# Attention in two halves a pair: four switches of TensorE's tiling, sums inverted one pair on, a new order of SyncE's transfers

## The chip, the core and the metric

The kernel runs on one core of a Trainium2 chip. A core has five engines that run side by side: TensorE (PE, matrix products; PEld is its loading of weights), VectorE (DVE), ScalarE (ACT), GpSimd (POOL) and SyncE (SP), which here only issues transfers (DMAs). PE's results go to PSUM, a small memory, and VectorE and ScalarE read them there. The other on-chip memory is SBUF, with 128 partitions. The metric is device time in microseconds; less is better.

## The reference

Two blocks follow each other. The first is attention with a hash mask, over 4 batches, 8 heads, 768 positions and a head size of 64; the second is a feed-forward over the 3,072 tokens of 512 that come out of it.

```python
q_bits = np.einsum('bhsd,dk->bhsk', q, proj) > 0        # 6 bits of a hash, for k too
mask = q_bucket[:, :, :, None] == k_bucket[:, :, None, :]
scores = np.where(mask, q @ k.T / sqrt(D), -1e9)
attn = exp(scores - max) / (sum + 1e-9)
x = attn @ v                                            # (B,H,S,D) -> (B*S, H*D)
h = x @ w_in                                            # 512 -> 2048
out = (h * sigmoid(1.702 * h)) @ w_out                  # 2048 -> 512
```

The weights of the feed-forward come as 64-bit floats and are converted on the chip.

## The kernel before

**Pairs.** Attention goes over 16 pairs of heads, n from 0 to 15, in the loop of `attention` that starts at line 648. The 128 partitions hold the two heads' 64 dimensions. Scores are made transposed: keys on the partitions, in six tiles of 128 keys (`kt`), queries along the row, in two halves of 384 (`c`). For a tile of keys and a half of queries, PE first adds a product of hash features (bf16; lines 497 and 514), which makes the masked ones hugely negative, and then the product of k and q. ScalarE takes the exponential of the result into `es[c]` (line 486).

**Tilings of PE.** PE can be split into independent smaller arrays. From pair 3 on (`BY_PARTS`), `scores_of_four` (line 500) makes two tiles of keys at once, a *group*: four products that each use 32 rows of the array (32*128 in the profile). For this a second copy of k and q exists, `other`, in which the halves of the dimensions are exchanged (`exchange`, line 439), and a second copy of the hash features (`spread`, line 479). Pairs 0 to 2 use 64 rows (64*128). The values (`values`, line 540), the hashes (`hashed`, line 455) and the sums of the exponentials (`total`, line 561) use 32 columns of the array (128*32). Each pass from one kind to the other switches the tiling.

**PSUM slots.** Scores, values, hashes and sums take turns in four slots of two 512-word places a partition (`in_turn`, line 310). One tile of keys takes a whole slot, values take half of one, and the hashes or the sums can take its other half. A slot can be used again when those that read it are done.

**One pair before.** PE's order in pair n is: two groups of scores; the values of the second half of pair n−1; two groups; the values of the first half of pair n; two groups; the hashes of pair n+2 and the sums of pair n−1. That is six switches. VectorE turns the raw k and q into columns (`turn`), adds up the exponentials (`add_high`; GpSimd adds the lower three tiles, `add_low`), makes the hash features from the hashes (`featured`), inverts the sums of pair n−2 (`invert`, line 571, which first transposes them, line 575, and then takes reciprocals) and multiplies the output by them (`norm`). It also converts one chunk of weights a pair, in six steps (`convert`, called by `begin` and `step`). ScalarE, beside the exponentials, unloads the values (`unload`, lines 558 and 559) and sums squares for a guard (`measure`, line 451).

**SyncE's row.** All transfers of attention but the weights' go through `load` (line 339, issued at line 340). SyncE issues them one after the other and waits at each for what it needs. A pair has 24: four for the next k, four for the next q (`fetch`), two for the values (`fetch_v`, one a head), eight for the hash features of pair n+1 (from `f` to their places, line 471), four for the exchange of halves of pair n+1 and two for the second copy of its features. The last two copy what the eight wrote, and wait until it has landed. From pair 2 on they are kept in the order of the program; before that the scheduler places them.

**Order.** The order of the work on PE, VectorE, ScalarE and GpSimd is that of the program text; a release of a buffer or slot is a wait on a semaphore. After attention comes the feed-forward, which uses products of the Strassen kind and is not touched by the change.

Of the kernel before, what the change touches and what calls it, by code (L numbers as in the profile page):

```python
# [38 lines left out]
def kernel(  # L39
# [249 lines left out]
    def attention(ff):  # L289
# [4 lines left out]
        with actx:  # L294
# [42 lines left out]
            turns_kept = [False]  # L337

            def load(out, in_):
                dma = nc.sync.dma_start(out=out, in_=in_)  # L340
                if turns_kept[0]:
                    tc.keep_in_program_order(dma)
                return dma
# [6 lines left out]
            def behind(x):  # L350

                nc.vector.memset(x, 0.0)

            def fetch(n, name):
# [3 lines left out]
                if (n, name) == (2, "q"):  # L358
                    behind(x[:, 0, 0:1])
# [7 lines left out]
            def fetch_v(n):  # L367
                b, hp = pairs[n]
                x = ld.tile([P, T, 2, D], F32, tag="v", name="v", bufs=2)
                if n == 0:  # L370
                    x = x.rearrange("p t j d -> p (t j d)").rearrange("p (j t d) -> p t j d", j=2, d=D)
                vts[n] = x
                if n == 1:
                    behind(x[:, 0, :, 0])
# [104 lines left out]
            def spread(n):  # L479

                exchange(n)
# [58 lines left out]
            def values(n, c, kts, at):  # L540
                av, vt = at[:, 0 : HS + 1], vts[n]
                avs[n, c] = av
                for t in kts:
                    row = t if n else 2 * (t % GT) + t // GT
                    for j in range(2):
                        for d in range(0, D, 32):
                            nc.tensor.matmul(av[D * j + d : D * j + d + 32, :], vt[:, row, j, d : d + 32], es[c][:, t, j, :],  # L547
                                             start=(t == 0), stop=(t == T - 1))
# [80 lines left out]
            fetch(2, "k")  # L629
            scores(0, 1, low, slots)  # L630
            turn(1, "q")
            add_high(0, 0)
            add_low(0, 1)
            measure(1, "q")
# [4 lines left out]
            fetch(2, "q")  # L639
            fetch_v(1)  # L640
            scores(0, 1, high, slots)
            measure(2, "k")
# [3 lines left out]
            turns[0] = 0  # L646
            inverse = {}
            for n in range(1, last + 1):

                more = n + 2 <= last  # L650
                if n > 1:
                    if n < last:
                        features = featured(n + 1)
                        next(features)
                    if n > 2:
                        inverse[n - 2] = invert(n - 2)
                        next(inverse[n - 2])
# [851 lines left out]
```

## Time and profile before

| | us |
|---|---|
| median of 3 runs | 859.17 |
| lowest and highest of them | 855.86, 860.81 |
| the profiled execution's own time | 857.29 |
| its span | 855.5 |

The clock granted to PE was 0.999 over the span. A row of the order of time shows the start and the length in us, the engine, the line, the operation, output and inputs, the shapes and the count; in brackets stands the idle time before it and what ended it. Neighbouring instructions of a kind are merged in one row. "s" is a PSUM slot, "feat" the hash features, "own" and "s_in" the columns of k and q and their exchanged copy (both names stand for either, since they rotate through three places), "e" the exponentials, "rt" the transposed sums, "acc" the added exponentials. SPq and ACTq rows are issues of DMAs.

| stretch of the span (us) | what is in it |
|---|---|
| 0 to 66.6 | pairs 0 to 2, without the 32-row tiling |
| 66.6 to 294.1 | pairs 3 to 14 |
| 294.1 to 317.4 | pair 15 and the last sums |
| 317.4 to 855.5 | feed-forward |

### The profile page before, as it was taken

Reading aid. Unit: us, or ns where it says so; the run is one execution under the profiler, and the core shown is the slowest. Engines: PE = TensorE matmul, PEld = TensorE weight load, DVE = VectorE, ACT = ScalarE, POOL = GpSimd, SP = SyncE. Lnnn points to the kernel's source line nnn. Section 1 sums busy time; section 2 is a strip of 40 time slices with the busy share of each in tenths; the row PEclk is TensorE's granted clock in tenths of the full one; section 3 lists DMA queues with packets and bytes.
Section 4 is the critical chain, followed back from the end, with each engine's and each line's share of the span. In section 5 each row is a group of like instructions: output and inputs, shape, how many; then the busy total and the mean of one; then the engine's idle time right before and its main releaser. Section 6 shows DMA issues by size and latency. Waiting matters only on the chain.

```text
span 855.5 us, 14892 instructions
## 1 busy us (share of the span) xinstructions
PE 843.9 (99%) x5595; PEld 524.7 (61%) x5595; DVE 683.9 (80%) x1069; ACT 337.6 (39%) x553; POOL 361.8 (42%) x321
## 2 busy tenths in 40 slices
PE   8999999999999999999999999999999999999997
PEld 4444444444444444565666666545888888888886
DVE  4479889988878986788887788676998977897786
ACT  6666665667666644343444444433000000000000
POOL 4333343433433448997854467568664100000000
PEclk9999999999999999999999999999999999999999
DMA  5657866776777403526466546577854675467534
GB/s 112 98 91 150 152 137 134 158 138 130 155 146 142 114 3 135 161 81 264 188 230 221 214 155 213 205 265 269 278 174 154 205 244 194 157 222 233 193 120 100
DMA packets 165197, 144.04 MB, mean 168 GB/s; under 512 B 124384, under 2 KB 139872, under 8 KB 159872
## 3 DMA queue, kind: packets, MB, share of 16 engines
q1 hardware_dynamic: 154640, 111.22, 47.6%
q10 hardware_dynamic: 10480, 31.81, 11.8%
q8 instruction: 45, 0.74, 0.4%
q14 instruction: 32, 0.26, 0.1%
HBM read 79.69 MB, written 50.33 MB: 152 GB/s over the span
## 4 chain that ended last, share of the span: by engine, by line
PE 89%; SPq 3%; DMA 3%; ACT 1%; DVE 1%; issue 1%; POOL 1%; ACTq 0%; DVEq 0%; POOLq 0%
PE product L1232 30%; PE product L905 23%; PE s L547 12%; PE s L514 12%; PE small L973 6%; SPq L340 3%; PE product L973 3%; DMA feat<-feat 1%; PE s L497 1%; DMA q<-in_q_dram 1%; ACT e L486 1%; PE s L569 1%; PE s L461 1%; DVE acc L538 0%; POOL above L334 0%
## 5 line engine op out<-in xcount | busy, mean ns | idle before, releaser
L486 ACT ACTIVATE e<-s 128x768 f32<-128x768 f32 x192 | 143.7, 812 | 62.2 <-PE s L514 46.6
L547 PE MATMUL s<-e,v 128*32 128x385 f32 x1536 | 131.6, 488 | 0.0
L525 POOL TENSOR_TENSOR t_x<-e 128x768 f32<-128x768 f32 x32 | 55.2, 1724 | 137.5 <-ACT e L486 132.0
L905 PE MATMUL product<-xT,w_in_sb 128*128 128x512 f32 x216 | 100.0, 593 | 0.1
L547 PEld LDWEIGHTS s<-e,v 128*32 128x32 f32 x1536 | 47.2, 109 | 79.1 <-issue 60.3
L905 PE MATMUL product<-t_x,s_in 128*128 128x512 f32 x192 | 89.5, 593 | 0.0
L514 PE MATMUL s<-s_in 32*128 32x384 f32 x816 | 79.9, 482 | 0.0
L525 POOL TENSOR_TENSOR t_x<-t_x,e 128x768 f32<-128x768 f32 x32 | 55.9, 1747 | 55.7 <-ACT e L486 54.6
L538 DVE TENSOR_TENSOR acc<-acc,e 128x768 f32<-128x768 f32 x63 | 73.6, 1168 | 2.8 <-ACT e L486 0.6
L1268 ACT COPY u<-product 128x256 f32<-128x256 f32 x20 | 7.4, 372 | 158.1 <-PE product L1232 124.9
L905 PEld LDWEIGHTS product<-xT,w_in_sb 128*128 128x128 f32 x216 | 41.0, 190 | 35.7 <-issue 32.7
L905 PEld LDWEIGHTS product<-t_x,s_in 128*128 128x128 f32 x192 | 36.5, 191 | 29.8 <-issue 26.7
L514 PEld LDWEIGHTS s<-s_in 32*128 32x128 f32 x816 | 41.1, 185 | 19.8 <-issue 1.9
L514 PE MATMUL s<-own 32*128 32x384 f32 x432 | 45.6, 487 | 0.0
L921 DVE TENSOR_TENSOR u<-product,u 128x256 f32<-128x256 f32 (+1 forms) x60 | 28.4, 486 | 15.5 <-PE product L973 12.9
L466 DVE TENSOR_SCALAR f<-s,above,weight 128x384 bf16<-128x384 f32 x15 | 10.1, 676 | 32.9 <-PE s L569 25.0
L1232 PE MATMUL product<-raw_g,xT 128*128 128x256 f32 x152 | 35.1, 380 | 0.0
L514 PE MATMUL s<-feat 32*128 32x384 bf16 x312 | 30.4, 327 | 2.5 <-DMA feat<-feat 2.0
L226 POOL TENSOR_TENSOR v<-c,v 128x1024 f32<-128x1024 f32 (+1 forms) x15 | 32.3, 2156 | 1.0
L225 POOL TENSOR_TENSOR u<-v,u 128x1024 f32<-128x1024 f32 (+1 forms) x11 | 23.8, 2166 | 20.2 <-ACT v L918 14.1
L921 DVE TENSOR_TENSOR v<-product,v 128x512 f32<-128x512 f32 x24 | 16.5, 689 | 19.5 <-PE product L905 19.5
L535 DVE SCALAR_TENSOR_TENSOR acc<-t_x,e 128x768 f32<-128x768 f32 x31 | 29.4, 947 | 3.1 <-ACT e L486 2.5
(298 smaller groups left out, 1801.1 us busy)
## 6 DMA issues: line engine op xcount, KB each, us to landing
raw_g<-g_dram SPq DMA_DIRECT2D x20, 1024.0 KB, 5.1
s_in<-g_dram SPq DMA_DIRECT2D x20, 1024.0 KB, 5.0
g_dram<-c ACTq DMA_DIRECT2D x18, 512.0 KB, 2.9
raw<-in_moe_w_out_dram ACTq DMA_DIRECT2D x16, 512.0 KB, 3.7
raw<-in_moe_w_in_dram ACTq DMA_DIRECT2D x15, 512.0 KB, 5.2
s_in<-own SPq DMA_DIRECT2D x36, 192.0 KB, 3.3
v<-in_v_dram SPq DMA_DIRECT2D x32, 192.0 KB, 3.8
k<-in_k_dram SPq DMA_DIRECT2D x60, 96.0 KB, 3.1
```

The source lines that it names most:

```text
L226: lambda: eng.tensor_tensor(b12, b22, b12, op=Alu.subtract),
L340: dma = nc.sync.dma_start(out=out, in_=in_)
L486: nc.scalar.activation(es[c][:, kt, :, 0:HS], ps[:, :, 0:HS], Act.Exp, scale=1.0 / D**0.5)
L514: nc.tensor.matmul(ps[i][:, j, 0:HS], a[r0 : r0 + 32, keys], m[r0 : r0 + 32, cols], start=at == 0, stop=at == 2)
L525: nc.gpsimd.tensor_tensor(low_sum, low_sum if i else e[:, 0], e[:, i + 1], op=Alu.add)
L535: nc.vector.scalar_tensor_tensor(acc, terms[0], T * TINY, terms[1], op0=Alu.add, op1=Alu.add)
L538: nc.vector.tensor_tensor(acc, acc, terms[i + 1], op=Alu.add)
L547: nc.tensor.matmul(av[D * j + d : D * j + d + 32, :], vt[:, row, j, d : d + 32], es[c][:, t, j, :], start=(t == 0), stop=(t == T - 1))
L905: nc.tensor.matmul(ps, wq[LEFT[i]][:, kc, :], xq[RIGHT[i]][:, kc, :], start=(start and kc == 0), stop=(kc == K2 - 1), skip_group_check=not ...
L921: nc.vector.tensor_tensor(dst, x, y, op=Alu.add)
L973: nc.tensor.matmul(x, wq[LEFT[i]], xq[RIGHT[i]], start=start, stop=True, skip_group_check=True)
L1232: nc.tensor.matmul(ps, wq[LEFT[i]][:, c, :], gq[RIGHT[i]][:, c, :], start=(onto is None and c == 0), stop=(c == F4 - 1), skip_group_check= ...
```

## The change

It rewrites the order of the loop over pairs, and of what precedes it.

- A pair has two halves: three groups of scores of the first half of queries, then the values of the second half of pair n−1 with the sums of pair n−1 behind them in the same slot; three groups of the second half, then the values of the first half of pair n with the hashes of pair n+2 behind them in the same slot. That is four switches of tiling.
- The sums of pair n−1 are inverted and applied in pair n, and not in pair n+1.
- k, q, their turns and their measures move to earlier places: `measure(n+3, "k")` at the end of pair n, both turns of pair n+2 near its start. The exchange of halves is made for pair n+2 and not for pair n+1 (`exchange` is called apart from `copied`, which is what is left of `spread`).
- The values of two heads come in one transfer, and lie as head, row, dimension in SBUF.
- All transfers of `load` are kept in the order of the program from the start. In a pair this is: eight features of pair n+1, k of n+3, two copies of features of n+1, q of n+3, values of n+1, exchange of n+2.
- The two memsets that held transfers back (`behind`) are gone.
- Before the loop, the hashes of pair 2 and the sums of pair 0 are made behind pair 0's last values.
- After the loop, the norm of pair 14 and the last step of the conversion are gone, since they are done in pair 15.

```diff
             def fetch_v(n):
                 b, hp = pairs[n]
...
-                for j in range(2):
-                    order = "(t p) d -> p t d" if n else "(p t) d -> p t d"
-                    load(x[:, :, j, :], v[b, 2 * hp + j].rearrange(order, p=P))
+                x = vts[n] = ld.tile([P, 2, T, D], F32, tag="v", name="v", bufs=2)
+                heads = v[b, 2 * hp : 2 * hp + 2]
+                if n:
+                    load(x.rearrange("p j t d -> p (j t) d"), heads.rearrange("j (t p) d -> p (j t) d", p=P))
...
-            def spread(n):
-
-                exchange(n)
+            def copied(n):
+
                 for j in range(2):
                     load(both[n % 2][D * j + 32 : D * j + 48], both[n % 2][D * j : D * j + 16])
...
+            hashed(2, at[:, 1])
+            at = place(0)
+            total(0, at[:, 0])
+            turns[0] = 1
             for n in range(1, last + 1):
...
+                scores_of_four(n, ((0, 0), (0, 2), (0, 4)))
+                add_low(n, 0)
+                if more:
+                    turn(n + 2, "k")
+                    turn(n + 2, "q")
...
+                    if more3:
+                        fetch(n + 3, "k")
+                    if BY_PARTS <= n + 1 <= last:
+                        copied(n + 1)
+                    if more:
+                        measure(n + 2, "q")
+                    if more3:
+                        fetch(n + 3, "q")
+                step(n, 2)
+                add_high(n, 0, (0,))
+                step(n)
+                if n > 1:
+                    at = in_turn()
+                    values(n - 1, 1, every, at[:, 0])
+                    total(n - 1, at[:, 1])
+                    unload(n - 1, 1)
+                    inverse = invert(n - 1)
+                    next(inverse)
+                if n < last:
+                    fetch_v(n + 1)
+                if more and n + 2 >= BY_PARTS:
+                    exchange(n + 2)
+                step(n, 2)
+                add_high(n, 0, (1,))
+                next(inverse)
+                scores_of_four(n, ((1, 0), (1, 2), (1, 4)))
+                add_low(n, 1)
+                norm(n - 1)
+                add_high(n, 0, (2,))
...
+                step(n)
+                at = in_turn()
+                values(n, 0, every, at[:, 0])
+                if more:
+                    hashed(n + 2, at[:, 1])
+                unload(n, 0)
```

More of the change, by code (lines that the diff above doesn't have):

```diff
@@ new lines, in attention @@
+                more, more3 = n + 2 <= last, n + 3 <= last
+                if n < last:
+                    features = featured(n + 1)
+                    next(features)
+                if n == 1:
+                    inverse = invert(0)
+                    next(inverse)
+                else:
+                    add_high(n - 1, 1)
+                chunk = begin(n)
+                if n < last:
+                    first = next(features)
+                    if chunk is not None:
+                        behind_issue(chunk, first)
+                        behind_issue(next(features), chunk)
+                    whole(features)
@@ L764, in attention @@
                 f()
-            norm(last - 1)
-            step(last)
             inverse = invert(last)
```

141 lines of the change are left out of this document (26 added, 115 removed).

## The prediction

> **What bounds the kernel now.** I read the page first, then the windows, then the order of time on each engine. The page's first part says that TensorE (PE) is never free; the windows then give the attention's pairs 3 to 13 (66.62 to 276.19), one undisturbed pair among them (12), and pair 14.
>
> ```profile
> span 855.5 us, 14892 instructions
> PE 843.9 (99%) x5595; PEld 524.7 (61%) x5595; DVE 683.9 (80%) x1069; ACT 337.6 (39%) x553; POOL 361.8 (42%) x321
> 66.62:276.19 209.57, 207.07 (x2556) 93.97 (x2553) 178.71 (x255) 138.89 (x231) 77.08 (x44) 1.00 0.75 145
> 239.16:257.68 18.52, 18.52 (x237) 8.29 (x234) 15.54 (x23) 12.60 (x22) 7.26 (x4) 1.00 0.73 144
> 276.19:294.07 17.88, 17.88 (x230) 8.02 (x227) 17.00 (x22) 10.43 (x17) 6.23 (x4) 1.00 0.45 110
> ```
>
> Columns: window, length, busy time of PE, PEld, DVE, ACT, POOL, granted clock, DMA share, GB/s. Eleven pairs at 18.52 would be 203.72; they took 209.57, so 5.85 us are waits. The largest is shown in PE's and SyncE's order of time: pair 7's scores wait for a copy of the hash features that SyncE issued only at 141.12.
>
> ```profile
> 144.52 0.67 PE L514 MATMUL s<-feat 32*128 32x384 bf16 x2 [2.02 <-DMA feat<-feat]
> ```
>
> ```profile
> 141.12 1.53 SPq L340 DMA_DIRECT2D feat<-feat  x2
> ```
>
> ```profile
> SPq L340 <- DMA q<-in_q_dram: 8.3, 11, 1.4
> ```
>
> The last row is of SyncE's waits (us, times, longest): its row is held up by loads of q that have not landed, and the features stand behind them.
>
> **Prices of the pieces on PE**, from one undisturbed pair and from pairs 2 and 15:
>
> ```profile
> 246.19 0.34 PE L514 MATMUL s<-feat 32*128 32x384 bf16 x4
> ...
> 247.66 0.33 PE L514 MATMUL s<-feat 32*128 32x384 bf16 x4
> ...
> 249.21 4.09 PE L547 MATMUL s<-e,v 128*32 128x385 f32 x48
> 253.23 0.34 PE L514 MATMUL s<-feat 32*128 32x384 bf16 x4
> ...
> 254.69 0.33 PE L514 MATMUL s<-feat 32*128 32x384 bf16 x4
> ...
> 256.25 0.52 PE L461 MATMUL s<-s_in,pf_k 128*32 128x384 f32 x2
> ...
> 256.92 0.83 PE L569 MATMUL s<-acc,ones 128*32 128x384 f32 x8
> 257.68 0.34 PE L514 MATMUL s<-feat 32*128 32x384 bf16 x4
> ```
>
> ```profile
> 45.17 0.52 PE L461 MATMUL s<-own,pf_k 128*32 128x384 f32 x2
> ...
> 45.96 0.80 PE L497 MATMUL s<-feat 64*128 64x384 bf16 x2
> ...
> 304.32 4.09 PE L547 MATMUL s<-e,v 128*32 128x385 f32 x48
> 308.22 0.83 PE L569 MATMUL s<-acc,ones 128*32 128x384 f32 x8
> ...
> 310.45 0.45 PE L514 MATMUL s<-feat 32*128 32x384 bf16 x4
> ...
> 312.11 4.09 PE L547 MATMUL s<-e,v 128*32 128x385 f32 x48
> ...
> 317.24 1.88 PE L905 MATMUL product<-xT,w_in_sb 128*128 128x512 f32 x4
> ```
>
> Starts subtracted: a group of scores (two tiles of keys) 1.46 (254.69 − 253.23); a group with the switch to another tiling behind it 1.55 (249.21 − 247.66), so that switch is 0.09; values followed by scores 4.02, values followed by sums in the same tiling 3.90, so the switch back is 0.12; hashes before sums 0.67, sums before scores 0.76, hashes before scores 0.79. A pair before is 3 × (1.46 + 1.55) + 2 × 4.02 + 0.67 + 0.76 = 18.50; the window says 18.52.
>
> **The change, part by part.**
>
> *Four switches.* A pair is now twice: three groups, then one set of values with the sums or the hashes straight behind it. 2 × (2 × 1.46 + 1.55) + 2 × 3.90 + 0.76 + 0.79 = 18.29. That saves 0.23 a pair, if nothing waits.
>
> *What waits then.* Scores rotate through four PSUM slots, two to a group, so a third group in a row needs the slots of the first, which ScalarE must have read. Before, values always stood between. ScalarE's order of time:
>
> ```profile
> 247.87 1.51 ACT L486 ACTIVATE e<-s 128x768 f32<-128x768 f32 x2 [0.77 <-PE s L514]
> ```
>
> The first group ends at 247.66 and both its exponentials are read at 249.38, 1.72 later. A third group wants its second slot 1.46 after the first group's end: 0.26 too early. A release takes some hundredths more: at 310.45 a group wanted a slot that VectorE's transpose left at 310.50 (row below), and its values came 1.66 behind it instead of 1.55, a wait of 0.11 where 0.05 was owed. So 0.31 a half, 0.62 a pair, and a pair is 18.91. The bounds: 0, if the pair of matmuls that needs no late slot hides it; and 0.48, if its four streams also fall out of step, by half of what the late ones at 144.52 lost (0.67 against the 0.34 at 246.19). I take the middle, whose rows are nearest.
> The Trainium skill, "TensorEngine Tiling (Array Packing)", section PSUM Bottleneck, warns that tiling speeds up TensorE and not the reading of PSUM, which may become the limit; it speaks against putting three groups in a row, and the row above agrees with it. By it the sum is the one below; were there slots enough it would be 846.5.
>
> *Sums inverted one pair on.* The denominators of pair n−1 are now summed behind the values of the same half, in the same PSUM tile; the transpose that reads them runs after ScalarE has unloaded the values. Pair 15 already does this:
>
> ```profile
> 309.92 0.58 DVE L575 STREAM_TRANSPOSE rt<-s 128x384 f32<-128x384 f32 x1 [0.42 <-ACT xT L559]
> ```
>
> It comes 0.93 after the scores' start (308.22 + 0.77 = 308.99) and frees the slot at 310.50, while the second group wants it at 310.45. The 0.05 to 0.11 is not added: the third group's wait counts from the exponentials, which do not move. The hash features now share such a tile too and so start 0.93 into the pair; the cover is the same wait, and the features have the rest of the pair to land. The work of VectorE is the same, 15.54 a pair; queued behind its transpose stand one step of the weights' conversion, one sum and the inversion, and PE waits for none of these.
>
> *SyncE's row; values in one transfer.* A pair issued 8 feature copies, 4 exchanges of halves, 2 copies of features, 4 + 4 of k and q, 2 of values: 24; now 23. From the listings of SyncE's line and of the issues:
>
> ```profile
> L340 SPq DMA_DIRECT2D feat<-f x96: 507/580/4372, 71.9 to 281.8; - x96
> ```
>
> ```profile
> q<-in_q_dram SPq DMA_DIRECT2D x44, 96.0 KB, 5.5
> feat<-f SPq DMA_DIRECT2D x96, 12.0 KB, 3.1
> feat<-feat SPq DMA_DIRECT2D x24, 48.0 KB, 3.2
> ```
>
> At 0.58 each that is 13.9 before and 13.3 after, and 0.58 saved is off the path as long as SyncE has slack. New order, from the pair's start: features 1.6 to 6.3 (their source is ready after 0.93 + 0.6); k to 8.6; the copies, which wait until the features have landed (6.3 + 3.1 = 9.4), to 10.6, landed 13.8; q to 12.9; values 13.5; the exchange of the pair after next, held by q's landing, until about 16.7. Scores need the copies at 18.9: 5 us to spare, where before the four transfers of the exchange stood between the features and these copies. The exchange gets a whole pair more. I therefore take the 5.85 us of waits as gone. If that cover fails, they come back.
>
> *The start.* The hashes of pair 2 and the denominators of pair 0 move ahead of pair 1, before whose scores the sums must be ready:
>
> ```profile
> 25.42 4.20 PE L547 MATMUL s<-e,v 128*32 128x385 f32 x48
> 29.55 0.34 PE L497 MATMUL s<-feat 64*128 64x384 bf16 x2
> ...
> 36.12 4.18 PE L547 MATMUL s<-e,v 128*32 128x385 f32 x46
> ...
> 54.50 0.34 PE L497 MATMUL s<-feat 64*128 64x384 bf16 x2
> ...
> 57.84 4.09 PE L547 MATMUL s<-e,v 128*32 128x385 f32 x48
> ```
>
> ```profile
> 28.47 2.02 DVE L538 TENSOR_TENSOR acc<-acc,e 128x768 f32<-128x768 f32 x2
> ```
>
> Eight untiled key tiles take 6.57, four 3.34, so each further one 0.81; twelve are 9.80 and six 4.96. Values from 25.42 to 29.43 (they took 0.11 too long there), hashes to 30.10, sums wait for VectorE's 30.49 (0.45 lost): 31.31; twelve tiles 41.11; values 45.01; hashes 45.80; six tiles 50.76; values 54.66; sums 55.42; six tiles 60.38; values and hashes 65.07. Pair 3 began at 66.62: 1.55 gained, its waits for features (at 45.96 0.80 stands for 0.34) among them.
>
> **The sum.** Start −1.55. Pairs 3 to 13: 11 × 18.91 = 208.01, −1.56. Pair 14 has no hashes: 18.91 − 0.79 + 0.12 = 18.24, +0.36. Pair 15, to the product at 317.24, was 23.17 and is 2 × (4.47 + 0.31) + 3 × 3.90 + 0.76 + (317.24 − 312.11 − 3.90 = 1.23) = 23.25, +0.08. The feed-forward behind it is the same. Together −2.7 on the profiled execution's 857.29: 854.6. That execution is 1.9 below the median of the runs shown (859.17), which spread from 855.86 to 860.81; late features are the likely part of that spread, so no offset is added.
>
> **The rivals.** Within 0.5% is 4.3 us, about what a measurement of this kernel can tell: 854.9 to 863.5.
> 1. *No wait for the third group.* For it: PE can run the half of the group whose slot is free. Against: matmuls go out in order, and at 310.45 the wait showed in full. 26 waits × 0.31 = 8.1 less: 846.5.
> 2. *The features stay late.* SyncE's waits are for landings, and the DMA share of 0.75 does not fall. The 5.85 comes back: 860.4. With uneven restarts alone (26 × 0.17) it would be 859.0. Against: 5 us of slack by the issues.
> 3. *Slower: VectorE becomes the bound.* Its adds stretch while GpSimd adds:
>
> ```profile
> 135.47 1.92 POOL L525 TENSOR_TENSOR t_x<-e 128x768 f32<-128x768 f32 x1 [4.65 <-ACT e L486]
> ```
>
> ```profile
> 135.91 2.30 DVE L538 TENSOR_TENSOR acc<-acc,e 128x768 f32<-128x768 f32 x1
> ...
> 139.02 0.91 DVE L538 TENSOR_TENSOR acc<-acc,e 128x768 f32<-128x768 f32 x1
> ```
>
> That is 1.39 lost. The transposes of a pair's sums must be out early in its second half, and of 18.91 VectorE works 15.54; of the 3.4 left some 1.2 (an estimate, from the 0.93 above and the feature's start) are pauses for PE that it can't use: 2.2 of slack. Two such losses a pair (2.78) exceed it by 0.6, and 13 × 0.6 brings 862.4; three (4.17) exceed it by 2.0: 880. It decides against the change from 2.9 a pair on. Against: the undisturbed pair's 15.54 has its stretches in already. The Trainium skill, "SBUF — State Buffer", section Who interferes with whom, calls this an exclusive lock for a whole instruction, which these rows bear out.
>
> **How the numbers follow.** My sum 0.52 (851 to 859 with its own bounds, and with its middle just at the edge of what can be told: 0.28 of it faster, 0.24 same); rival 1 0.12, faster; rival 2 0.21, same; rival 3 0.15, slower. Faster 0.40, same 0.45, slower 0.15. The range goes from rival 1's 846.5 to 862, past rival 2, and leaves out most of rival 3.
>
> **What would show it.** Undisturbed pairs of 18.9 with no wait for a DMA; the third group of a half starting 0.3 late, and values 4.8 after a half's start; pair 3 at 65.1; SyncE idle some 2 us before each row of features. A pair of 18.3 is rival 1; PE waiting on features, rival 2; VectorE without idle time before its hash features, rival 3. Wrong too, if the feed-forward does not take the same time.

## The result, and the profile after

The changed kernel takes 862.33 us (median; 861.49 to 865.63), the kernel before, run on the same chip between its runs, 858.33. The ratio is 1.0051 with an interval of 1.0027 to 1.0076: slower by half a per cent. The prediction said 854.6 with a range that ended at 862.0, and gave "slower" 0.15. The profiled execution took 863.15.

The page's first part after the change, to be set beside that of before:

```profile
span 861.3 us, 14838 instructions
PE 847.7 (98%) x5595; PEld 529.3 (61%) x5595; DVE 691.8 (80%) x1067; ACT 342.3 (40%) x553; POOL 368.4 (43%) x321
```

The windows (length, busy time by engine, granted clock, DMA share, GB/s) of pairs 3 to 13, of one undisturbed pair, of pair 14, of the first half of pair 2, and of 3.41 us in that half:

```profile
71.81:281.32 209.51, 209.51 (x2556) 98.22 (x2553) 189.22 (x253) 141.21 (x229) 80.37 (x44) 1.00 0.68 142
128.95:148.00 19.05, 19.05 (x237) 8.94 (x235) 17.20 (x23) 12.90 (x21) 7.31 (x4) 1.00 0.71 147
281.32:300.08 18.76, 18.37 (x229) 8.75 (x226) 17.54 (x22) 11.04 (x17) 7.88 (x4) 1.00 0.25 62
48.34:57.51 9.17, 6.72 (x41) 3.30 (x37) 4.77 (x6) 4.36 (x7) 2.51 (x2) 0.82 1.01 181
...
54.19:57.60 3.41, 3.41 (x16) 1.58 (x19) 0.98 (x1) 2.76 (x4) 2.60 (x2) 0.50 0.88 221
```

By stages, from the starts of PE's work:

| | before | predicted | after |
|---|---|---|---|
| pair 3 begins | 66.62 | 65.07 | 71.81 |
| pairs 3 to 13 | 209.57 | 208.01 | 209.51 |
| pair 14 | 17.88 | 18.24 | 18.76 |
| pair 15, to the first product | 23.17 | 23.25 | 23.06 |
| feed-forward | 538.26 | 538.26 | 538.16 |

The eleven middle pairs, at which the change aims, take what they took before; they have no wait for transfers any more, but each is 0.53 longer than an undisturbed pair of before. The loss is in the start. PE's order of time there:

```profile
32.44 0.52 PE L448 MATMUL s<-s_in,pf_k 128*32 128x384 f32 x2 [1.94 <-ACT xT L545]
...
54.19 0.50 PE L483 MATMUL s<-feat 64*128 64x384 bf16 x2 [2.45 <-ACT e L472]
54.46 1.51 PE L483 MATMUL s<-s_in 64*128 64x384 f32 x4
```

and ScalarE's, which both waits name:

```profile
29.47 0.86 ACT L438 ACTIVATE xT<-k 128x768 f32<-128x768 f32 x1
...
30.45 0.84 ACT L438 ACTIVATE xT<-q 128x768 f32<-128x768 f32 x1
...
31.46 0.93 ACT L545 ACTIVATE xT<-s,vs 128x384 f32<-128x384 f32 x1
...
52.89 0.34 ACTq L165 DMA_DIRECT2D raw<-in_moe_w_in_dram  x1
53.33 3.62 ACT L472 ACTIVATE e<-s 128x768 f32<-128x768 f32 x5 [4.09 <-DMA k<-in_k_dram]
```

The first wait: the hashes of pair 2 share a PSUM tile with the last values of pair 0 and are written in the program behind the unload of these values; the unload stands on ScalarE behind two measures. The second: ScalarE stands at the issue of the first chunk of weights until a load of pair 4's k has landed (at 52.87), with exponentials behind it, and PE has no free slot. When PE goes on, its clock is halved for 3.41 us (the last window; the row of 1.51 above has four streams that take 0.81 otherwise).

ScalarE stood at that issue before the change just as long:

```profile
52.40 0.35 ACTq L165 DMA_DIRECT2D raw<-in_moe_w_in_dram  x1
52.86 1.51 ACT L486 ACTIVATE e<-s 128x768 f32<-128x768 f32 x2 [3.80 <-DMA k<-in_k_dram]
```

There PE lost nothing, because it was in the values from 50.48 to 54.50. The change put the values behind all six tiles of the half, so that the cover came too late.

### The profile page after: what moved, and what is told of

Its sections match the earlier page's. It is cut to its first block, busy times and chain, and to the rows that moved or that the text cites. A ratio compares the mean times of both kernels' runs of the same rounds, so it can differ in the third digit from the quotient of the medians.

```text
span 861.3 us, 14838 instructions
## 1 busy us (share of the span) xinstructions
PE 847.7 (98%) x5595; PEld 529.3 (61%) x5595; DVE 691.8 (80%) x1067; ACT 342.3 (40%) x553; POOL 368.4 (43%) x321
## 4 chain that ended last, share of the span: by engine, by line
PE 93%; ACT 2%; DVE 2%; DMA 1%; POOL 1%; issue 1%; SPq 0%; ACTq 0%; POOLq 0%; DVEq 0%
PE product L1190 29%; PE product L863 22%; PE s L500 14%; PE s L533 14%; PE small L931 6%; PE product L931 3%; PE s L483 2%; ACT e L472 1%; PE s L555 1%; PE s L448 1%; DMA k<-in_k_dram 1%; DVE acc L524 0%; SPq L339 0%; DVE t_x L225 0%; ACT xT L545 0%
## 5 line engine op out<-in xcount | busy, mean ns | idle before, releaser
L472 ACT ACTIVATE e<-s 128x768 f32<-128x768 f32 x192 | 145.9, 810 | 38.4 <-PE s L500 23.6
L500 PE MATMUL s<-s_in 32*128 32x384 f32 x816 | 83.2, 485 | 0.0
L511 POOL TENSOR_TENSOR t_x<-t_x,e 128x768 f32<-128x768 f32 x32 | 62.3, 1946 | 2.5
L500 PEld LDWEIGHTS s<-s_in 32*128 32x128 f32 x816 | 45.1, 185 | 14.1 <-issue 0.2
L500 PE MATMUL s<-own 32*128 32x384 f32 x432 | 49.2, 496 | 0.0
L500 PEld LDWEIGHTS <-feat 32*128 32x128 bf16 x312 | 13.4, 92 | 43.1 <-issue 37.9
L500 PE MATMUL s<-feat 32*128 32x384 bf16 x312 | 37.6, 326 | 0.5 <-DVE rt L561 0.4
L879 DVE TENSOR_TENSOR c<-small,c 128x256 f32<-128x256 f32 (+1 forms) x54 | 24.2, 462 | 9.2 <-PE small L931 9.0
```

The lines of the kernel that those rows point to most:

```text
L472: nc.scalar.activation(es[c][:, kt, :, 0:HS], ps[:, :, 0:HS], Act.Exp, scale=1.0 / D**0.5)
L500: nc.tensor.matmul(ps[i][:, j, 0:HS], a[r0 : r0 + 32, keys], m[r0 : r0 + 32, cols], start=at == 0, stop=at == 2)
L511: nc.gpsimd.tensor_tensor(low_sum, low_sum if i else e[:, 0], e[:, i + 1], op=Alu.add)
L879: nc.vector.tensor_tensor(dst, x, y, op=Alu.add)
```

## The experiments

Times and ratios are against runs of the kernel before on the same chip (medians 856.9 to 857.9; the changed kernel's own ratio was 1.0051); pairs are read from the traces, one execution of each kernel.

### Is the pair's extra time the third group's wait?

The exponentials of a half's first two tiles are taken for one head only, so that ScalarE hands these slots back earlier; the other head's part is left out:

```diff
-                        weigh(n, c, k0 + i, ps[i])
+                        weigh(n, c, k0 + i, ps[i], 1 if k0 == 0 else 2)
```

> The changed kernel with the exponentials of the first two tiles of keys of each half made for one head only from pair 3 on (the other head's exponentials of these tiles stay those of an earlier pair, so that part of the attention is left out). ScalarE then has read the slots of a half's first group 0.8 us earlier. Theory A (the third group of a half waits for ScalarE's reading of the first group's second slot): the 0.39 us that a half loses falls to what its second group waits for its slot, 0.15 in the first half and 0.05 in the second, so a pair goes from 19.05 to about 18.5 and the kernel loses some 7 us. Rival C (the loss is PE's own: three groups in a row without a change of tiling run out of step): a pair stays at 19.05.

Measured, in a single execution: 856.17. First PE's order in an undisturbed pair of the changed kernel (starts of the three groups, of the values, and the same in the second half):

```profile
128.95 0.34 PE L500 MATMUL s<-feat 32*128 32x384 bf16 x4
...
130.41 0.54 PE L500 MATMUL s<-feat 32*128 32x384 bf16 x4
...
132.02 0.56 PE L500 MATMUL s<-feat 32*128 32x384 bf16 x4
...
133.81 4.09 PE L533 MATMUL s<-e,v 128*32 128x385 f32 x48
...
138.47 0.34 PE L500 MATMUL s<-feat 32*128 32x384 bf16 x4
...
139.94 0.45 PE L500 MATMUL s<-feat 32*128 32x384 bf16 x4
...
141.45 0.66 PE L500 MATMUL s<-feat 32*128 32x384 bf16 x4
...
143.33 4.09 PE L533 MATMUL s<-e,v 128*32 128x385 f32 x48
```

then the first half of this experiment:

```profile
125.44 0.34 PE L500 MATMUL s<-feat 32*128 32x384 bf16 x4
...
126.90 0.54 PE L500 MATMUL s<-feat 32*128 32x384 bf16 x4
...
128.50 0.39 PE L500 MATMUL s<-feat 32*128 32x384 bf16 x4
...
130.11 4.09 PE L533 MATMUL s<-e,v 128*32 128x385 f32 x48
```

In the changed kernel the third group takes 1.79 and 1.88 (133.81 − 132.02, 143.33 − 141.45) where 1.55 is due, the second 1.61 and 1.51 where 1.46 is due: 0.39 too much in each half. With less work for ScalarE the third group falls to 1.61, the pair to 18.60. So 0.45 a pair is ScalarE's release of the slots, shown. The 0.15 in front of the second group stays. It belongs to the slot that the values share with the hashes, or with the sums in the second half: in the changed kernel VectorE reads that slot until 130.57 and 139.99, and the second group wanted it at 130.41 and 139.94. VectorE's and ScalarE's order of time there:

```profile
129.89 0.68 DVE L453 TENSOR_SCALAR f<-s,above,weight 128x384 bf16<-128x384 f32 x1 [1.31 <-ACT xT L545]
...
139.41 0.58 DVE L561 STREAM_TRANSPOSE rt<-s 128x384 f32<-128x384 f32 x1 [0.25 <-ACT xT L545]
```

```profile
130.69 4.69 ACT L472 ACTIVATE e<-s 128x768 f32<-128x768 f32 x6 [0.83 <-PE s L500]
...
140.21 3.02 ACT L472 ACTIVATE e<-s 128x768 f32<-128x768 f32 x4 [0.83 <-PE s L500]
```

In the changed kernel this delay adds nothing to the time: it is 0.15 in one half and 0.05 in the other, and both halves lose the same 0.39. The third group's late slot counts from the first group's exponentials, and these begin 1.74 after the half's start in both (128.95 to 130.69, 138.47 to 140.21). The delay shows only where ScalarE is quicker, as in this experiment.

### Can the start be put right?

Three kernels, one edit, the other, and both. The first puts the hashes ahead of the unload:

```diff
-            unload(0, 1)
             hashed(2, at[:, 1])
+            unload(0, 1)
```

> The changed kernel with pair 2's hashes put ahead of ScalarE's unload of pair 0's second values instead of behind it. Theory A (the time before pair 3 is lost to PE waiting for ScalarE in two places): the 1.9 us wait of PE ahead of these hashes goes, PE waits only for the sums of pair 0 (VectorE, ready at 31.4), pair 1 starts 1.6 us earlier than 33.87, and the kernel is 1.6 us faster than the changed one, about 860.7. Rival B (the start is bound by the landing of k and q, and every wait taken away comes back at the next one): pair 3 starts at 71.8 as before and the time stays 862.3.

The second issues the first chunk of weights at the end of pair 1:

```diff
-                chunk = begin(n)
+                chunk = None if n == 2 else begin(n)
...
                 if n == 1:
+                    begin(2)
                     for x in "kq":
                         measure(3, x)
```

> The changed kernel with the first chunk of weights issued one pair earlier, at the end of pair 1's exponentials, instead of ahead of pair 2's. Theory A: ScalarE no longer stands 4.1 us at this issue, PE's wait of 2.5 us in pair 2 goes and with it the 3.4 us of half clock that follow it, pair 2 takes 19.3 instead of 23.5 and the kernel is 4.2 us faster than the changed one, about 858.1. Rival B: pair 2 still waits, for q of pair 4 or the features of pair 3, and the time stays within 1 us of 862.3. If only the wait and not the clock counts, the gain is 2.5.

> The changed kernel with both of these edits. Theory A: the gains add, 5.8 us less than the changed kernel, 856.5, which is about 2 us below the kernel before; pair 3 starts at 66.0. Rival B: little is gained, above 860.

Measured: 862.51 (ratio 1.0058, 1.0037 to 1.0079), 863.57 (1.0067, 1.0046 to 1.0087) and 860.97 (1.0034, 1.0015 to 1.0052). PE's largest wait in the start, in the three kernels in turn:

```profile
53.72 0.51 PE L483 MATMUL s<-feat 64*128 64x384 bf16 x2 [4.60 <-ACT e L472]
```

```profile
63.88 0.34 PE L483 MATMUL s<-feat 64*128 64x384 bf16 x2 [3.34 <-DVE rt L561]
```

```profile
61.05 0.34 PE L483 MATMUL s<-feat 64*128 64x384 bf16 x2 [2.94 <-DVE rt L561]
```

The gain of each edit showed at its own place (pair 1 began 2.6 earlier in the first, of which 0.96 is that its first scores began earlier; the first half of pair 2 ran without a wait in the second) and was gone some microseconds on. With the hashes early, PE comes sooner to ScalarE's wait for k. With the chunk early, PE comes to a transposition of sums that stands on VectorE behind the turn of pair 4's q; VectorE's order of time in the second kernel:

```profile
59.57 0.98 DVE L424 STREAM_TRANSPOSE own<-q 128x768 f32<-128x768 f32 x1 [1.65 <-DMA q<-in_q_dram]
```

So the fourth mend adds to both that it turns that q half a pair later, with its measure, the next load of q and the exchange:

```diff
                     turn(n + 2, "k")
-                    turn(n + 2, "q")
+                    if n != 2:
+                        turn(n + 2, "q")
...
                 next(inverse)
+                if n == 2:
+                    turn(4, "q")
                 scores_of_four(n, ((1, 0), (1, 2), (1, 4)))
```

> The changed kernel with three edits: pair 2's hashes ahead of ScalarE's unload, the first chunk of weights issued one pair earlier, and, new, in pair 2 alone the turn of pair 4's q put behind the inversion of the sums instead of near the pair's start (its measure, the load of pair 5's q and pair 4's exchange follow it). Theory A2 (the start is a chain of engines that stand in order at work whose load has not landed: first ScalarE at the chunk, then VectorE at the turn of q, and PE waits for whatever stands behind): with the turn out of the way the transposed sums are in time, the wait of 2.9 us in pair 2's second half goes with the half clock behind it, pair 3 starts at 65.5 instead of 69.9 and the kernel is 4.3 us faster than with the first two edits alone, 856.7, level with the kernel before. Rival B (the loads bound the start whatever stands in front): pair 3 starts at 69.9 still, about 861.

Measured: 860.43 (1.0034, 1.0014 to 1.0053). Pair 3 began at 66.36, 5.45 sooner than in the changed kernel; but ScalarE then stood at the second chunk, in pair 3:

```profile
71.17 0.34 PE L500 MATMUL s<-feat 32*128 32x384 bf16 x2 [1.05 <-ACT e L472]
```

```profile
69.87 0.33 ACTq L165 DMA_DIRECT2D raw<-in_moe_w_in_dram  x1
```

The fifth keeps the early hashes and the late q, and issues the first two chunks behind the exponentials of their half:

```diff
-                chunk = None if n == 2 else begin(n)
+                chunk = None if n in (2, 3) else begin(n)
...
                 scores_of_four(n, ((0, 0), (0, 2), (0, 4)))
+                if n in (2, 3):
+                    begin(n)
```

> The changed kernel with its start mended as in the run that turned pair 4's q later (hashes of pair 2 ahead of the unload, pair 4's q in the second half of pair 2), but the first two weights chunks (pairs 2 and 3) are issued on ScalarE behind the exponentials of the pair's first half, so that no exponential stands behind an issue that waits for a landing. Theory: pair 3 again begins at about 66.4, and the 1.4 that PE waited for ScalarE in pair 3 (issue of the second chunk at 69.87, exponentials after 3.06 idle) are gone; pairs of 19.05 from there. Pair 4 at about 86, that is 1.6 below the 860.4 of that run: 858.8, and what is then left over the kernel before with the new row and the values in one transfer (856.4) is 11 times the 0.5 of the undisturbed pair less the start's gain. Rival: the start's wait moves once more, to a later pair: 860.4 or more.

Measured: 862.03 (1.0072, 1.0048 to 1.0095). The rival held. The chunk now lands late, VectorE's conversion waits for it, and the transposed sums behind that conversion hold PE:

```profile
81.68 0.34 PE L500 MATMUL s<-feat 32*128 32x384 bf16 x2 [2.90 <-DVE rt L561]
```

Of the 6.7 between the predicted and the measured start of pair 3, the best of these mends kept 3.2 up to pair 5 (106.66 instead of 109.90), and 0.78 of that is that the first scores began at 9.77 instead of 10.55. Each took its own wait away and made or uncovered another.

### The parts of the change alone, on the kernel before

The new order of SyncE's row alone (the exchange of pair n+2 behind q, the copies behind k; the first exchange in pair 1); the values in one transfer alone; both:

```diff
                         if n + 1 >= BY_PARTS:
-                            spread(n + 1)
...
                     if n + 3 <= last:
                         fetch(n + 3, "k")
+                    if BY_PARTS <= n + 1 <= last:
+                        copied(n + 1)
...
                         fetch(n + 3, "q")
+                    if n > 1:
+                        exchange(n + 2)
...
+                    exchange(3)
                     fetch(4, "k")
```

```diff
-                for j in range(2):
-                    load(x[:, :, j, :], v[b, 2 * hp + j].rearrange(order, p=P))
+                    load(x.rearrange("p j t d -> p (j t) d"), heads.rearrange("j (t p) d -> p (j t) d", p=P))
```

> The kernel before, six switches of tiling and all, with only this of the change: the exchange of halves is issued for pair n+2 behind the load of q, and the two copies of the features behind the load of k, so that the features stand first in SyncE's row. Theory D (the new row alone takes away the waits for features, 5.85 us in pairs 3 to 13 of the profiled execution): pairs 3 to 13 take 18.5 each, 204 in all instead of 209.6, and the kernel is 5 us faster than before, about 852. Rival E (the waits are for landings in busy DMA queues and come back whatever the order): pairs 3 to 13 take 207 or more and the time is within 2 us of 857.2.

> The kernel before with only this of the change: the values of two heads in one transfer. SyncE has 0.5 us less to issue in each pair. Theory D gives a fraction of the waits for features back, 0 to 2 us faster than 857.2. If the larger transfer holds up the loads behind it, 0 to 2 us slower.

> The kernel before with both: the new place of exchange and copies in SyncE's row and the values in one transfer. Theory D: about 852, and if SyncE has no slack with the new row alone, 0.5 to 1 us below it. Rival E: within 2 us of 857.2.

Measured: the row alone 855.71 (ratio 0.9975, 0.9961 to 0.9990), faster than both kernels and the fastest by ratio here; the values alone 865.04 (1.0090, 1.0057 to 1.0122); both 856.36 (0.9991, 0.9968 to 1.0015). The window of pairs 5 to 13 with the row alone:

```profile
107.19:273.85 166.66, 166.66 (x2094) 74.36 (x2091) 139.97 (x207) 113.70 (x190) 65.81 (x36) 1.00 0.69 147
```

That is nine pairs at 18.52, and no wait for a transfer: the row does what the prediction said of it, and it does so without the change of tiling. Of the values alone only the fastest execution, 859.47, has a profile; it shows waits for the copies of features, one of which halves the clock. Why the others are slower still is open. Under the new row the merged transfer makes no difference that can be told from zero.

In the start the row alone lost 2.3 (pair 3 at 68.91): ScalarE stood at the first chunk until 55.51. Two kernels placed the first exchange elsewhere, behind pair 4's loads and behind pair 3's features:

```diff
-                    exchange(3)
                     fetch(4, "k")
...
                             fetch(4, "q")
+                            exchange(3)
                         first = next(features)
```

> The kernel before with the new order of SyncE's row, as in the run with that alone, but the first exchange of halves (for pair 3) is issued behind the loads of pair 4's k and q and no longer ahead of them. Theory: in the run with the new row alone ScalarE stood at the issue of the first weights chunk until 55.51, 7.1 us, because pair 4's k was issued 2.4 us later (51.02 against 48.93) behind the exchange; PE lost 1.8 + 0.3 in pair 2 and pair 3 began at 68.91 instead of 66.62. With k issued at about 48.9 the chunk goes out at about 52.4, pair 3 begins at about 66.6, the undisturbed pairs stay 18.5, and the time is 2.3 below the 855.7 of that run: 853.4. Rival: what is taken out there comes back in pair 3, as it did when the start of the changed kernel was mended: 855.7.

```diff
-                    exchange(3)
                     fetch(4, "k")
...
                         whole(features)
+                        if n == 2:
+                            exchange(3)
```

> The kernel before with the new order of SyncE's row, but the first exchange of halves (for pair 3) is issued behind the features of pair 3, where the kernel before had it, and the copies behind the load of k. The earlier exchange that went behind pair 4's loads did not help: k was issued at 48.96 and still the chunk's issue on ScalarE came at 55.48. Theory: that issue waits for the landing of the transfer that was issued eight transfers before it in the order of the program, whatever it is. Eight before the chunk stood pair 4's k in the kernel before (chunk at 52.40), the same k, issued 2.1 later, in the run with the new row alone (55.51), and, with the four transfers of the exchange between, pair 4's q in the last one (55.48). Here it is pair 4's k at about 48.9 again: chunk at about 52.4, no wait of PE on ScalarE in pair 2, pair 3 at 66.6, pairs of 18.5 from pair 4 on, 853.4. Rival, that ScalarE waits for something else or that the time comes back in pair 3: chunk at 55.5, pair 3 at 68.8, 855.5.

Measured: 855.39 (0.9985, 0.9969 to 1.0002) and 857.35 (0.9989, 0.9967 to 1.0011). SyncE's and ScalarE's issues, first kernel and second:

```profile
48.96 2.22 SPq L340 DMA_DIRECT2D k<-in_k_dram  x4
51.29 2.43 SPq L340 DMA_DIRECT2D q<-in_q_dram  x4
```

```profile
55.48 0.34 ACTq L165 DMA_DIRECT2D raw<-in_moe_w_in_dram  x1
```

```profile
52.46 0.35 ACTq L165 DMA_DIRECT2D raw<-in_moe_w_in_dram  x1
```

My theory for the first fell: k went out at 48.96, as before the change, and ScalarE still stood until 55.48. The second bears out what I put in its place, that the issue waits for the landing of the transfer eight before it in the program's order: with the exchange's four between, that is pair 4's q; without them it is k, and the issue is at 52.46 and pair 3 at 66.33. The traces also record what ties the two together: each of these transfers tells of its landing by one of eight semaphores, which they take in turn, and a chunk's issue that had to wait starts just after the transfer before it on the same semaphore has landed. That is k at 52.38 and the issue at 52.40 in the kernel before, k at 52.44 and the issue at 52.46 in the second kernel here, q at 55.46 and the issue at 55.48 in the first. SyncE's own issues wait in the same way. In pairs 3 to 13 of the kernel before, ten issues of features began 0.06 after the landing of the q with their semaphore, and had waited 6.9 us for it in all; with the row alone and in the changed kernel there is no such wait. So this is the holdup by q that the prediction read in SyncE's waits.

But then pair 3 of the second kernel waited for its copies, issued behind pair 5's k (at 65.56, where the kernel before had 63.75), and ran 3.41 at half its clock:

```profile
69.00 0.61 PE L513 MATMUL s<-feat 32*128 32x384 bf16 x2 [2.34 <-DMA feat<-feat]
```

Two more moved the change-over of the row: copies of pair 3 too at their old place, and the new row from pair 5 on only:

```diff
                             exchange(3)
+                            copied(3)
...
-                    if BY_PARTS <= n + 1 <= last:
+                    if BY_PARTS < n + 1 <= last:
```

> As the run with the exchange behind pair 3's features, with pair 3's copies too where the kernel before had them, straight behind that exchange and ahead of pair 5's k: the new row rules from pair 3 on. In that run the copies were issued at 65.56, two transfers of 2.8 later than in the kernel before (63.75), TensorE waited 2.34 for them in pair 3 and then ran 3.4 at half its clock, while pairs 4 to 13 took 18.5 each. Theory: every loss of the start is one transfer that is issued too late, so with the copies at about 62.7 pair 3 begins at 66.5 and pair 4 at 85.3 instead of 89.48, and the time is 853.4. Rival, a fixed loss that goes where the row is tightest: pair 4 begins at 88 or later and the time is 855.5 or more.

```diff
-                        if n + 1 >= BY_PARTS:
-                            spread(n + 1)
+                        if BY_PARTS <= n + 1 <= 6:
+                            exchange(n + 1)
+                        if BY_PARTS <= n + 1 <= 5:
+                            copied(n + 1)
...
+                    if n >= 5:
+                        exchange(n + 2)
```

> The kernel before with the old row up to pair 4 and the new row (exchange of the pair after next behind q, copies behind k) from pair 5 on; in pair 5 SyncE issues two exchanges. Theory: the new row costs the start one exchange that has to be issued a pair earlier (4 issues, 2.5 us) while SyncE has no pause, which is why pair 5 began at 107.1 to 108.0 in all four runs with the new row instead of 104.79, whatever was moved; later, the row has 3 us of pause a pair and takes it. Then pair 5 begins at about 104.8, from pair 6 or 7 on a pair takes 18.5, pair 14 begins at about 272 instead of 273.85, and the time is 853.5 to 854. Rival: SyncE never pauses in the old row either, so the two exchanges of pair 5 push the rest back just as far: pair 7 at 144.2, pair 14 at 273.8, 855.7.

Measured: 856.55 (0.9979, 0.9962 to 0.9997) and 857.38 (1.0003, 0.9983 to 1.0023). In the first, pair 3 began at 66.65 and pair 4 at 87.02, and then pair 4 waited, so that the rival's time held (855.5 or more):

```profile
88.66 0.78 PE L513 MATMUL s<-feat 32*128 32x384 bf16 x2 [1.30 <-DMA feat<-feat]
```

Pair 5 began at 107.61. In five kernels with the new row from the start on it began at 107.1 to 108.1 (104.79 before), whichever wait was taken out. The last is inconclusive: the execution that was profiled, 854.08, goes as the theory says (pair 5 at 104.29, pair 14 at 272.96), but it is the fastest of twelve that reach to 859.15, and of the others there is no profile.

### The start of before with the pairs of the change

Pairs 0 to 2 are those of the kernel before, with the first exchange behind pair 3's features; pairs 3 to 15 are those of the changed one, and the values come in one transfer throughout. The second kernel has the copies of pair 3 straight behind that exchange. In the diff the body of the first loop is that of the kernel before:

```diff
+            for n in (1, 2):
...
-            for n in range(1, last + 1):
+            for n in range(3, last + 1):
...
+                if n == 3:
+                    next(inverse)
+                    norm(1)
+                    measure(5, "k")
                 if more:
                     turn(n + 2, "k")
```

> Pairs 0 to 2 in the order of the kernel before (with the values in one transfer and the first exchange behind pair 3's features), pairs 3 to 15 in the order of the changed kernel. Theory: the changed kernel is slower by two separate things, its start (pair 3 at 71.81 instead of 66.62) and undisturbed pairs of 19.05 instead of 18.5. Here the start is that of before: pair 3 at about 66.6, 11 pairs at 19.05 to 276.2, pair 14 and 15 as in the changed kernel, product at 318 instead of 323.1: 857.2 with the changed kernel's 862.3. Rival: the waits of the start come back in pair 3 or 4, as in every mend so far: 859 to 862.

> As the run with the start of before and the pairs 3 to 15 of the changed kernel, with pair 3's copies straight behind the exchange (in that run issued at 66.98, and pair 3 waited 2.85 for them, then 1.79 for ScalarE, which stood at the second chunk until 73.92). Theory: pair 3 begins at about 67 and loses no time to copies; what stands at the second chunk depends on pair 5's q, which doesn't move, so up to 1.8 may stay. Pair 4 begins at 86.1 to 87.9 instead of 91.67, and the time is 858 to 861, of which 11 pairs at 0.53 make 5.8 over the new row on the kernel before. Rival: pair 4 begins at 90 or later, 863 or more.

Measured: 864.28 (1.0081, 1.0050 to 1.0112) and 866.22 (1.0099, 1.0075 to 1.0124), no faster than the changed kernel itself, whose interval ends at 1.0076; the first is above what theory and rival said, the second is as the rival said. Pair 3 began at 67.14 and 67.32; pair 4 only at 91.67 and 93.75. The windows of pairs 4 to 13, ten at 19.05 each:

```profile
91.67:282.15 190.48, 190.48 (x2326) 89.32 (x2323) 172.04 (x230) 128.35 (x208) 73.12 (x40) 1.00 0.68 142
```

```profile
93.75:284.22 190.47, 190.47 (x2326) 89.34 (x2323) 172.05 (x230) 128.28 (x208) 73.09 (x40) 1.00 0.67 140
```

and in the second one's pair 3 ScalarE and PE:

```profile
73.62 0.33 ACTq L165 DMA_DIRECT2D raw<-in_moe_w_in_dram  x1
74.06 2.92 ACT L483 ACTIVATE e<-s 128x768 f32<-128x768 f32 x4 [7.23 <-DMA q<-in_q_dram]
```

```profile
74.92 0.50 PE L511 MATMUL s<-feat 32*128 32x384 bf16 x2 [4.50 <-ACT e L483]
```

So the pair's 19.05 doesn't depend on the start, and the start's loss is not taken away by the pairs 0 to 2 of before: it comes in pair 3, where the new order now begins. Pair 3 takes 24.5 and 26.4. In the first kernel PE waits 2.85 there for the copies and 1.79 for ScalarE, in the second 4.70 for ScalarE alone, with the clock halved from 73.75 to 80.58. ScalarE stands at the issue of the second chunk: eight transfers before it lies pair 5's q (one copy of features, four of the exchange, and then q's), which landed at 73.54 in the second kernel, and the issue is at 73.62. The theory for these two runs, that each late transfer can be taken away by itself, fell.

## Why the prediction was wrong

Before the chip ran, I made the sum 854.6; the profiled execution took 863.15. The 8.5 between them, by the prediction's steps:

**The start (predicted −1.55, measured +5.19): 6.7 of the 8.5.** This is the step that failed. I laid out PE's work with prices for every part and let only one wait into it, that of the sums for VectorE, which didn't show. Missing are three things, of which the trace of before showed the second, and a fourth that is chance:
- The hashes share a tile with values whose unload stands behind two measures: PE began pair 1 at 33.87 where the sum, shifted by 0.88 (below), gives 32.19, so 1.68.
- ScalarE's stand at the first chunk (3.80 idle, in the trace of before, off PE's path there): 2.45. I moved the values away from that place and didn't ask what they had been covering.
- The clock after that wait: 3.41 at half, 1.7.
- And 0.88 that has nothing to do with the change, bad luck of this execution against the one of before: the first scores began at 10.55 in this execution and anywhere between 9.59 and 10.56 in those of the other kernels, at which nothing was changed there.

Together 6.7. That the start's waits move on when they are taken away is shown by five kernels; that a chunk's issue waits for the transfer eight before it is shown by the two that changed which one that was, and by the semaphores. What stays open is why five different starts with the new row lose 2.3 to 3.3 by pair 5. Their traces name different waits: 1.3 to 1.9 for ScalarE at the first chunk in three of them, 2.34 and 1.30 for copies of features in the other two. It may be the one exchange (2.49 of issues) that has to go out a pair sooner while SyncE has no pause, which has about that size; the kernel made to show it was inconclusive.

**A pair: 18.91 predicted, 19.05 measured; 1.5 over eleven.** The mechanism was right: no wait for a DMA, values 4.86 behind a half's start (I had said 4.8), and a third group that ScalarE's reading of the first group's slots holds up. The size of that term was too low, 0.39 a half where I had put 0.31: the first group's second slot is read 1.79 after the group's end (130.41 to 132.20), where I took 1.72 from the kernel before. The sentence by which the shared tile costs nothing, because the third group's wait covers it, held: its 0.15 and 0.05 in front of the second group are part of the 0.39 and not on top of it. Rival 1 (no such wait, 846.5) is out.

**SyncE's row and the features: right.** No wait for features is left in pairs 3 to 13. SyncE's order of time shows the pause before them that I asked for, 2.9 where I had said 2 (143.11 + 3.66 to 149.64):

```profile
130.59 4.96 SPq L339 DMA_DIRECT2D feat<-f  x8
...
143.11 3.66 SPq L339 DMA_DIRECT2D s_in<-s_in  x4
149.64 3.25 SPq L339 DMA_DIRECT2D feat<-f  x4
```

Rival 2 is out. The row alone brought less than these 5.85, since it lost 2.3 in the start: 0.25% by ratio. I had put the spread of the kernel before down to late features; the row alone spreads over 1.3 (855.25 to 856.52), the kernel before on the same chip over 9.1, which fits. It doesn't show it: no slow execution of the kernel before has a profile, and its fastest (851.53) lies below all of the row alone.

**The switches: right.** With the third group less hindered a pair is 18.60, and its 0.31 above 18.29 is accounted for by the shared tile, which shows there (0.15 and 0.05), and by 0.06 behind each third group. The 0.23 saved is less than the 0.78 that the order of three groups costs.

**Pair 14: 0.52 too little.** It has a wait for the transposed sums that I had put at nothing:

```profile
293.05 0.34 PE L500 MATMUL s<-feat 32*128 32x384 bf16 x2 [0.39 <-DVE rt L561]
```

**Pair 15 and the feed-forward: right within 0.2.**

**Rival 3** came near in number (862.4) but not in kind: in the undisturbed pair VectorE works 17.20 of 19.05, 1.66 more than before, mostly from adds that stretch, and PE waits for none of these there. It is in the start that VectorE and ScalarE are late, and they are late because they stand at transfers.

## What to carry to other kernels

Before a block that keeps the bound engine busy without needing the others (here 4 us of values) is moved, list what the other engines wait for during it: those waits are free only there, and the profile of before shows them as idle time of engines that look uncritical. Engines that work in order pass on one late landing to everything behind it, an issue of a DMA included, so a wait removed at one place should be followed to the next one before it is counted as a gain. Where transfers take semaphores in turn, look up which transfer lies one full turn before an issue: its landing is a wait that stands in no line of the program. When a change has several parts, try the one that costs no order of work (here the row of transfers) by itself.

## What the runs showed of the hardware

A short wait of PE can cost more than its length, and the length alone doesn't tell when. After waits of 1.47, 2.34, 2.45, 2.94 and 3.34 the granted clock was 0.50 for some 3.41 us, and around one of 4.60 and one of 4.50 for 6.83; after waits of 2.02 (kernel before), 2.30 (one head's exponentials), 2.85 and 2.90 it was 1.00. The shortest, with the values alone on the kernel before, with the window behind it (0.50, third number from the end), and the window behind the wait of 2.90, in the kernel with both chunks late (1.00):

```profile
164.77 0.69 PE L513 MATMUL s<-feat 32*128 32x384 bf16 x2 [1.47 <-DMA feat<-feat]
```

```profile
166.41:169.82 3.41, 3.41 (x29) 1.77 (x22) 3.30 (x9) 1.51 (x2) 1.26 (x1) 0.50 1.16 191
```

```profile
81.68:85.09 3.41, 3.41 (x46) 2.16 (x49) 3.38 (x4) 2.47 (x5) 2.52 (x2) 1.00 0.73 120
```

The Trainium skill, "TensorE: Matmul & The Clock Gate", section What's actually happening, says that the activity is judged over windows of 3413 ns that run freely; the lengths of 3.41 and 6.83 agree with it. Its section Why this matters for your kernels counts only gaps above some 3 us as harmful; here one wait of half that was followed by a half clock, and others of up to 2.90 were not.

An issue of a DMA on ScalarE's queue waited for the landing of a transfer from SyncE's queue that has nothing to do with it, the eighth before it in the program, with which it shares one of eight semaphores. It came 0.02 after that landing: at 52.40 and 52.46 where that was k, and at 55.48 where it was q.
